# Pooled attention and a tanh-shrink layer: softmax with the row maximum, tokens on partitions, in place of keys on partitions

## The chip, the core and the metric

The kernel runs on one core of a Trainium2 chip. The metric is the device time of one execution in microseconds (us). The core has five engines with queues of their own: TensorE (PE) multiplies matrices, with the weight loads (PEld) beside it, VectorE (DVE) and ScalarE (ACT) work on rows, GpSimd (POOL) does the same more slowly, and SyncE (SP) issues most transfers. Sixteen DMA engines carry the transfers of all queues. PSUM, where matmuls write, has eight banks of 128 partitions by 512 fp32 columns.

## The reference

Inputs are q, k and v of shape (8 batches, 8 heads, 576 tokens, 64) and two weight matrices, 512 x 2048 and 2048 x 512, all fp32. What is computed, cut to its core:

```
k_p = k.reshape(B, H, 72, 8, D).mean(axis=3)        # 576 keys pooled to 72
v_p = v.reshape(B, H, 72, 8, D).mean(axis=3)
scores = q @ k_p.T / sqrt(D)
scores = scores - max(scores, axis=-1)
attn = exp(scores);  attn = attn / (sum(attn, axis=-1) + 1e-9)
x = (attn @ v_p)  ->  (B * S, H * D) = (4608, 512)
h = x @ w_in;  g = h - tanh(h);  out = g @ w_out
```

## The kernel before, in words

All matmuls take bf16 and add in fp32. The two large layers work in nine groups of 512 consecutive tokens (`TG`, `NG`). A group's **first layer** (`mlp_h_mms`, L448) makes 16 hidden blocks of 128: four matmuls of 512 columns each into one of three banks, w_in as weights and the transposed activations `xT` as moving operand. ACT takes tanh into `t_sb` (L464), and DVE subtracts it from the PSUM copy and writes `gT` (L466). The **second layer** (`mlp_o`, L475) takes four blocks of 128 tokens in turn, each 16 matmuls in four units of four; ACT copies the finished bank (L490) and SP stores it.

`xT` holds all 4608 tokens. A batch has 576, so groups and batches do not coincide: group g reads tokens of one or two batches, and the attention of batch g + 1 is worked out during group g.

Attention of one batch. The eight raw rows of each key are added in pairs, three adds (`pool_k`, L215; `pool_v`, L237), on POOL but for the first batches. 576 (head, key) rows lie in five tiles, and `KB` holds them so that one matmul serves two heads. **Scores have keys on partitions** (`score_mms`, L316): KB is the weight operand, the transposed queries `qT` move. ACT takes exp straight from PSUM into `E` (L340, L351), with the scale and without a maximum. `E` is then the weight operand of the matmuls with V (`av_mms`, L361), six of 130 columns for a block of 128 tokens. V has an extra column, so that the sum of weights comes out beside each head; DVE takes its reciprocal (L385) and multiplies (L386). The block `x_sb` is turned into `xT` by a DMA transpose (L403), or by TensorE (L409) in the first two batches.

The order is written out by hand: the schedule is manual, each engine runs its instructions in the order in which the program names them. During group g the program puts, between the second layer's units u = 0 to 15, the scores after u = 1 to 5, the blocks of x after u = 7, 8, 9, 10 and 12, and the cast and the five DMA transposes of the following batch's q after u = 12 (L809 to L823). Loads of the batch after next and the transpose of k come in the first layer (L796 to L808). SP's queue carries all these loads, transposes and stores in the same order.

Before group 0 comes an opening (L562 to L743). k, q and v of batch 0 arrive in pieces, POOL starts the loads of w_in and w_out that cast to bf16 (L526, L533), DVE pools k, TensorE turns k and q against `ident` (L282, L194) and runs matmuls on zeros (`warm_pe`, L548) in between. Scores and exp go tile by tile as k arrives. V of batch 0 is pooled by TensorE (L642). Then x of batch 0 is made in pairs of blocks (`av_pair`, L686; L692), turned by TensorE and copied to xT by ACT (`x0_turn`, L699; L712), and the first matmuls of the first layer (`h_open`, L717) take only half of the contraction, for which x is ready first. In group 0's second layer batch 1's k, q and x are turned by TensorE too (L768 to L786).

Of the kernel before, what the change touches and what calls it, by code (L numbers as in the profile page):

```python
# [11 lines left out]
ALU = mybir.AluOpType  # L12
PSUM = bass.MemoryType.PSUM

B, H, S, D = 8, 8, 576, 64
POOL = 8
# [6 lines left out]
T = B * S  # L23
# [3 lines left out]
NG = T // TG  # L27
NT = 5
D1 = D + 1
PR = 2 * G  # L30
LO = PR - 128
KP = 160
NM = 4
# [4 lines left out]
def kernel(  # L38
# [14 lines left out]
    raw = ctx.enter_context(tc.tile_pool(name="raw", bufs=2))  # L53
    work = ctx.enter_context(tc.tile_pool(name="work", bufs=2))
    gpool = ctx.enter_context(tc.tile_pool(name="gpool", bufs=1))
# [3 lines left out]
    PS = psum.tile([128, 8, 512], FP32, name="PS")  # L59

    def bank(i, shape):
        n = 1
        for d in shape[1:]:
            n *= d
        v = PS[:, i, 0:n]
        if len(shape) == 3:
            return v.rearrange("p (a b) -> p a b", a=shape[1])
        if len(shape) == 4:
            return v.rearrange("p (a b c) -> p a b c", a=shape[1], b=shape[2])
        return v  # L70

    class Banks:
        def __init__(self, *ids):
            self.ids, self.n = ids, 0

        def tile(self, shape, dtype=None, name=None, tag=None):
            self.n += 1
            return bank(self.ids[(self.n - 1) % len(self.ids)], shape)

    ps_h = Banks(0, 1, 2)  # L80
    ps_o = Banks(3, 4)
    ps_a = Banks(5, 6, 7)

    ctx.enter_context(tc.manual_schedule())
# [5 lines left out]
    k_pairs = k_rows.rearrange("b (t r) n -> b r t n", r=PR)  # L90
    v_pairs = v_rows.rearrange("b (t r) n -> b r t n", r=PR)

    w1b = const.tile([128, NFB, DFF], BF16, name="w1b")
    w2b = const.tile([128, NHID, DM], BF16, name="w2b")
    xT = const.tile([128, NFB, T], BF16, name="xT")
    ident = const.tile([128, 128], BF16, name="ident")
    spread = const.tile([128, 128], BF16, name="spread")
    mask = const.tile([128, 3 * NM, 1], FP32, name="mask")
    k_raw = [const.tile([128, NT, POOL * D], FP32, name=f"k_raw{i}") for i in range(2)]
    v_raw = [const.tile([128, NT, POOL * D], FP32, name=f"v_raw{i}") for i in range(2)]  # L100
    KB = [const.tile([128, NM * KP], BF16, name=f"KB{i}") for i in range(2)]
    q_bf = const.tile([128, R + 1, H, D], BF16, name="q_bf")
    warm = const.tile([128, 1], FP32, name="warm")
    x0 = const.tile([128, 4, 2, 4, D], BF16, name="x0")
    VB = [const.tile([128, 3 * NM, D1], BF16, name=f"VB{i}") for i in range(2)]

    q_raws = {}
    rot = [0]

    def ps_any(shape, dtype, name):  # L110
        pool, tag = [(ps_a, "ps_a"), (ps_h, "hT_ps")][rot[0] % 2]
        rot[0] += 1
        return pool.tile(shape, dtype, name=name, tag=tag)

    evac_n = [0]

    def evac(out, in_, eng=None):
        if (evac_n[0] % 2) if eng is None else eng == "act":
            nc.scalar.copy(out=out, in_=in_)
        else:  # L120
            nc.vector.tensor_copy(out=out, in_=in_)
        evac_n[0] += 1

    def load_main(src, dst, b, t0, t1):
        return nc.sync.dma_start(out=dst[:, t0:t1, :], in_=src[b, 0:128, t0:t1, :])

    def load_left(src, dst, b, eng=nc.sync):
        return [
            eng.dma_start(out=dst[32 * t : 32 * t + LO, NM, :], in_=src[b, 128:PR, t, :])
            for t in range(NM)  # L130
        ]

    def load_dense(src, dst, b, eng=nc.sync):
        return eng.dma_start(
            out=dst[0 : NM * LO, NM, :], in_=src[b, 128:PR, :, :]
        )

    def load_k(b):
        return [
            load_main(k_pairs, k_raw[b % 2], b, 0, NM),  # L140
            load_dense(k_pairs, k_raw[b % 2], b),
        ]

    def load_v(b):
        return [load_main(v_pairs, v_raw[b % 2], b, 0, NM)] + load_left(
            v_pairs, v_raw[b % 2], b
        )

    def load_q_tail(b, t, eng):
        eng.dma_start(  # L150
            out=t[:QT, :, R, :], in_=q[b, :, QA:S, :].rearrange("h p d -> p h d")
        )

    def load_q(b, tail=True):
        if b not in q_raws:
            q_raws[b] = raw.tile([128, H, R + 1, D], FP32, name="q_raw", tag="q_raw")
        t = q_raws[b]
        nc.sync.dma_start(
            out=t[:, :, 0:R, :], in_=q[b, :, 0:QA, :].rearrange("h (p j) d -> p h j d", j=R)
        )  # L160
        if tail:
            load_q_tail(b, t, nc.sync)

    qTs = {}
    kdups = {}

    def q_cast(b, eng=nc.gpsimd.tensor_copy, parts=1):
        t = q_raws.pop(b)
        n = H // parts
        for h in range(0, H, n):  # L170
            eng(  # L171
                out=q_bf[:, 0:R, h : h + n, :].rearrange("p j h d -> p h j d"),
                in_=t[:, h : h + n, 0:R, :],
            )
        eng(out=q_bf[:QT, R, :, :], in_=t[:QT, :, R, :])

    def q_dma_transpose(b):
        qT = work.tile([128, NHP, S], BF16, name="qT", tag="qT")
        for j in range(R + 1):
            rows = 128 if j < R else QT  # L180
            nc.sync.dma_start_transpose(
                out=qT[:, :, j * 128 : j * 128 + rows],
                in_=q_bf[:rows, j, :, :].rearrange("p h d -> p (h d)"),
            )
        qTs[b] = qT

    def q_pe_transpose(b, hps, eng=None):
        if b not in qTs:
            qTs[b] = work.tile([128, NHP, S], BF16, name="qT", tag="qT")
        qT = qTs[b]  # L190
        for hp in hps:
            ps = ps_any([128, QA], FP32, "qT_ps")
            for j in range(R):
                nc.tensor.matmul(  # L194
                    ps[:, j * 128 : (j + 1) * 128],
                    lhsT=q_bf[:, j, 2 * hp : 2 * hp + 2, :].rearrange("p h d -> p (h d)"),
                    rhs=ident[:, :],
                    start=True,
                    stop=True,
                )  # L200
            evac(qT[:, hp, 0:QA], ps[:, :], eng)

    def q_pe_tail(b):
        ps = ps_any([128, NHP, QT], FP32, "qt_ps")
        for hp in range(NHP):
            nc.tensor.matmul(
                ps[:, hp, :],
                lhsT=q_bf[:, R, 2 * hp : 2 * hp + 2, :].rearrange("p h d -> p (h d)"),
                rhs=ident[:, 0:QT],
                start=True,  # L210
                stop=True,
            )
        evac(qTs[b][:, :, QA:S], ps[:, :, :])

    def pool_k(b, eng, t0=0, t1=NT, mid=()):  # L215
        r = k_raw[b % 2].rearrange("p t (j d) -> p t j d", d=D)[:, t0:t1, :, :]
        if b not in kdups:
            kdups[b] = work.tile([128, NT, 2, D], BF16, name="kd", tag="kd")
        kd = kdups[b][:, t0:t1, :, :]
        n = t1 - t0  # L220
        first = eng.tensor_tensor(  # L221
            out=r[:, :, 0:4, :], in0=r[:, :, 0:4, :], in1=r[:, :, 4:8, :], op=ALU.add
        )
        for c in mid:
# [629 lines left out]
```

## Time and profile before

| what | value |
|---|---|
| time, three runs | 301.23 us median (300.78 to 301.84) |
| span of the profiled execution, first to last instruction | 299.0 us |
| time of that execution around its span | not given apart |
| PE busy | 291.5 us (97%), 1672 matmuls |
| PEld / DVE / ACT / POOL busy | 142.8 / 158.4 / 148.8 / 115.7 us |
| granted TensorE clock | 1.000 |
| mean DMA rate | 167 GB/s; 49.79 MB moved |
| DMA queue of SP and ACT's hardware (q1) | 55.5% of 16 engines' span |
| first matmul of the first layer | 18.35 us |
| first matmul of group 1's first layer | 54.87 us |
| last matmul of the second layer's last 128 tokens | about 295 us |

Busy time counts an instruction from its start to its end; matmuls overlap, so their mean duration (379 ns for 512 columns) is longer than the step from one to the next. "Idle before" in a group's line is the engine's idle time just ahead of such instructions, and what ended most of it. The chain is followed back from the last instruction to whatever released each step. SPq is SyncE's queue, with the time that an issue takes.

### The profile page before, as it was taken

To read this page: it belongs to the slowest core of one execution; us is meant where nothing else is said; L and a number is where in the kernel's file an instruction comes from. 1 tells how busy PE (TensorE), PEld (TensorE's weight loads), DVE (VectorE), ACT (ScalarE), POOL (GpSimd) and SP (SyncE) were. 2 spreads that over 40 slices of the span, in tenths; PEclk is the share of its full clock that TensorE was granted. 3 is DMA by queue.
4 is the path that set the end of the run, shared out by engine and by line. 5 is a ranking of instruction groups with operands and counts; after the bars stand their busy time and mean duration, and the time that the engine had idled before them with its cause. 6 is when DMAs were issued, how large, how long until landed. Compare 5 with 4: busy or idle time off the path is not lost.

```text
span 299.0 us, 4704 instructions
## 1 busy us (share of the span) xinstructions
PE 291.5 (97%) x1672; PEld 142.8 (48%) x1672; DVE 158.4 (53%) x336; ACT 148.8 (50%) x279; POOL 115.7 (39%) x110
## 2 busy tenths in 40 slices
PE   7999999999999999999999999999999999999994
PEld 3454355544544454445544554455445544444443
DVE  5658665673547444753476247715680758008600
ACT  4647583666146623664266416651666066126511
POOL 8600906770396109913971099208930000000000
PEclk9999999999999999999999999999999999999999
DMA  7999999749955995699648974895431630111033
GB/s 259 221 211 280 310 235 328 233 89 331 233 109 109 290 283 129 109 297 250 105 89 236 313 166 88 265 294 137 89 66 35 90 96 0 37 70 36 2 70 70
DMA packets 66183, 49.79 MB, mean 167 GB/s; under 512 B 39920, under 2 KB 52976, under 8 KB 66160
## 3 DMA queue, kind: packets, MB, share of 16 engines
q1 hardware_dynamic: 58832, 42.94, 55.5%
q0 software_dynamic: 4752, 4.72, 9.5%
q10 hardware_dynamic: 2576, 1.84, 2.2%
q8 instruction: 13, 0.21, 0.3%
q14 instruction: 10, 0.08, 0.1%
HBM read 36.70 MB, written 9.44 MB: 154 GB/s over the span
## 4 chain that ended last, share of the span: by engine, by line
PE 85%; DMA 9%; POOL 4%; issue 0%; SPq 0%; ACT 0%; DVE 0%; POOLq 0%; DVEq 0%
PE PS L481 40%; PE PS L453 37%; DMA w1b<-in_moe_w_in_dram 4%; PE PS L368 4%; DMA k_raw<-in_k_dram 4%; PE PS L321 3%; POOL k_raw L221 1%; DMA out_dram<-o_sb 1%; POOL k_raw L226 1%; POOL kd L229 1%; POOL w2b L535 0%; PE PS L416 0%; POOL v_raw L599 0%; PE PS L194 0%; POOL w1b L528 0%
## 5 line engine op out<-in xcount | busy, mean ns | idle before, releaser
L481 PE MATMUL PS<-w2b,gT 128*128 128x512 bf16 x560 | 134.3, 379 | 0.0
L466 DVE TENSOR_TENSOR gT<-PS,t_sb 128x512 bf16<-128x512 f32 x144 | 98.9, 691 | 56.9 <-ACT t_sb L464 56.7
L453 PE MATMUL PS<-xT,w1b 128*128 128x512 bf16 x576 | 126.8, 379 | 0.6 <-ACT xT L712 0.6
L464 ACT ACTIVATE t_sb<-PS 128x512 f32<-128x512 f32 x144 | 85.6, 597 | 38.5 <-PE PS L453 37.7
L453 PEld LDWEIGHTS <-w1b 128*128 128x128 bf16 x576 | 55.9, 98 | 67.3 <-issue 0.8
L481 PEld LDWEIGHTS <-gT 128*128 128x128 bf16 x560 | 52.5, 98 | 52.0 <-issue 1.4
L490 ACT COPY o_sb<-PS 128x512 f32<-128x512 f32 x33 | 19.3, 586 | 75.2 <-PE PS L481 75.2
L385 DVE RECIPROCAL rden<-PS 128x4 f32<-128x4 f32 x72 | 12.8, 177 | 52.6 <-PE PS L368 52.3
L171 POOL CAST q_bf<-q_raw 128x2048 bf16<-128x2048 f32 x6 | 11.3, 1890 | 60.2 <-issue 34.2
L386 DVE TENSOR_TENSOR x_sb<-PS,rden 128x256 bf16<-128x256 f32 x72 | 30.6, 424 | 2.9 <-DMA xT<-x_sb 0.4
L221 POOL TENSOR_TENSOR k_raw<-k_raw 128x1280 f32<-128x1280 f32 x7 | 20.2, 2887 | 26.5 <-DMA k_raw<-in_k_dram 26.5
L340 ACT ACTIVATE E<-PS 128x288 bf16<-128x288 f32 x60 | 21.4, 409 | 13.2 <-PE PS L321 13.0
L368 PEld LDWEIGHTS <-E 128*128 128x128 bf16 x240 | 16.8, 98 | 8.3 <-issue 0.4
L368 PE MATMUL PS<-VB,E 128*128 128x130 bf16 x240 | 20.2, 220 | 0.1
L239 POOL TENSOR_TENSOR v_raw<-v_raw 128x1280 f32<-128x1280 f32 x6 | 17.4, 2900 | 0.0
L321 PE MATMUL PS<-qT,KB 128*128 128x288 bf16 (+5 forms) x128 | 17.0, 289 | 0.2
L321 PEld LDWEIGHTS <-KB 128*128 128x128 bf16 (+1 forms) x128 | 7.0, 96 | 10.2 <-issue 3.5
L550 PE MATMUL PS<-xT 128*128 128x512 bf16 x30 | 10.4, 463 | 1.3 <-DVE xT L562 1.3
L229 POOL TENSOR_TENSOR kd<-k_raw 128x640 bf16<-128x640 f32 x7 | 10.8, 1539 | 0.5
L226 POOL TENSOR_TENSOR k_raw<-k_raw 128x640 f32<-128x640 f32 x7 | 10.8, 1542 | 0.5
L242 POOL TENSOR_TENSOR v_raw<-v_raw 128x640 f32<-128x640 f32 x6 | 9.2, 1538 | 0.5
L272 POOL COPY KB<-kT 64x288 bf16<-64x288 bf16 x6 | 2.5, 418 | 13.8 <-DMA kT<-kd 13.8
(78 smaller groups left out, 107.1 us busy)
## 6 DMA issues: line engine op xcount, KB each, us to landing
k_raw<-in_k_dram SPq DMA_DIRECT2D x7, 1024.0 KB, 5.9
q_raw<-in_q_dram SPq DMA_DIRECT2D x7, 1024.0 KB, 10.2
v_raw<-in_v_dram SPq DMA_DIRECT2D x7, 1024.0 KB, 9.2
out_dram<-o_sb SPq DMA_DIRECT2D x38, 128.0 KB, 2.4
out_dram<-o_sb SPq DMA_DIRECT2D x16, 256.0 KB, 2.8
w1b<-in_moe_w_in_dram POOLq DMA_DIRECT2D x4, 512.0 KB, 13.7
w2b<-in_moe_w_out_dram POOLq DMA_DIRECT2D x4, 512.0 KB, 16.8
k_raw<-in_k_dram SPq DMA_DIRECT2D x7, 128.0 KB, 5.9
```

The source lines that it names most:

```text
L221: first = eng.tensor_tensor(out=r[:, :, 0:4, :], in0=r[:, :, 0:4, :], in1=r[:, :, 4:8, :], op=ALU.add)
L226: eng.tensor_tensor(out=r[:, :, 0:2, :], in0=r[:, :, 0:2, :], in1=r[:, :, 2:4, :], op=ALU.add)
L239: eng.tensor_tensor(out=r[:, :, 0:4, :], in0=r[:, :, 0:4, :], in1=r[:, :, 4:8, :], op=ALU.add)
L321: nc.tensor.matmul(dst[p : p + w], lhsT=KB[b % 2][:, o : o + w], rhs=qTs[b][:, m, c0:c1], start=True, stop=True,)
L340: nc.scalar.activation(out=E[:, t, half * hs : (half + 1) * hs], in_=ps[:, :], func=ACT.Exp, scale=SCALE)
L368: nc.tensor.matmul(ps[:, 2 * n : 2 * n + 2, :].rearrange("p h d -> p (h d)") if n < 2 else ps.rearrange("p (a s) d -> p a s d", s=2)[:, :, ...
L386: nc.vector.tensor_tensor(out=x_sb[:, half, :, :], in0=ps[:, :, 0:D], in1=rden[:, :, :].to_broadcast([128, 4, D]), op=ALU.mult,)
L453: nc.tensor.matmul(h_tiles[i][:, :], lhsT=w1b[:, fb, i * 128 : (i + 1) * 128], rhs=xT[:, fb, tok0 : tok0 + TG], start=(fb == 0), stop=(fb ...
L464: nc.scalar.activation(out=t_sb[:, :], in_=h_ps[:, :], func=ACT.Tanh)
L466: nc.vector.tensor_sub(out=gT[:, :], in0=h_ps[:, :], in1=t_sb[:, :])
L481: nc.tensor.matmul(o_ps[:, :], lhsT=gts[i][:, tb * 128 : (tb + 1) * 128], rhs=w2b[:, i, :], start=(i == 0), stop=(i == NHID - 1),)
L490: (nc.vector.tensor_copy if g == 0 and tb % 2 else nc.scalar.copy)(out=o_sb[:, :], in_=o_ps[:, :])
```

## The change

Most of the kernel is written anew; inputs, outputs, types, the pooling, the two layers' matmuls and the last 128 tokens' split store stay.

- **Groups.** Groups 0 to 7 are the first 512 tokens of one batch each; group 8 is the last 64 tokens of all eight batches. `xT` of all tokens becomes two buffers of 512 tokens in turn, and `xTt` for group 8. Tails of q are loaded, cast, turned and worked on for two batches together (`s_tail`, `av_tail`), in the group before an odd batch.
- **Scores** have tokens on partitions: `qT` is the weight operand, `KB` (144 columns for two heads) moves; four matmuls for 128 tokens, into two banks.
- **Row maximum.** DVE takes the maximum over 72 keys (L249) and subtracts it, from PSUM into an fp32 tile in SBUF (L252); ACT takes exp of that tile (L260).
- **Weights turned.** The matmul with V needs the weights with keys on partitions: a DMA transpose of 128 x 640 on SP's queue turns them (L273), in batch 0 TensorE and an ACT copy (L276).
- **V** matmuls are of 130, 195 and 65 columns (table `AV`); one reciprocal and one multiplication serve a whole block of 128 tokens, two banks at once.
- **Casts and turns.** The cast of q goes from POOL to ACT, in two pieces; one DMA transpose turns the 512 tokens of q, where there were five. Batch 1's q, k and first three x blocks are turned by DMA and not by TensorE.
- **Banks and order.** The first layer cycles through six banks (three before). The second layer's units are reordered, so that the last gT tiles are read later. Scores start in the first layer of the group, and the last block of x comes after unit 10, the tail after unit 13.
- **Opening.** The first layer of group 0 goes in halves of 256 tokens, two hidden blocks to a bank, and starts when two blocks of x are there. All of k is placed before the first scores. 28 matmuls on zeros stand in the opening (`fill`), 30 before.

```diff
+    def s_mms(unit, banks):
+        for ps, qT, kb in unit:
+            for m in range(NHP):
+                nc.tensor.matmul(PS[ps, banks[m // 2], KP * (m % 2) : KP * (m % 2) + KP],
+                    lhsT=qT[:, m, :], rhs=KB[kb][:, m, :], start=True, stop=True)
+    def s_shift(banks):
...
+        nc.vector.reduce_max(out=mx.rearrange("p k h o -> p k (h o)"), in_=sc, axis=AX.X)
+        nc.vector.tensor_tensor(out=sh[:, :, :, :], in0=sc,
+            in1=mx.to_broadcast([128, 2, 4, G]), op=ALU.subtract)
+    def s_exp(sh):
...
+        nc.scalar.activation(out=E[...], in_=sh[...], func=ACT.Exp, scale=SCALE)
+    def e_turn_dma(E):
...
+        nc.sync.dma_start_transpose(out=ET[:, :, :], in_=E.rearrange("p t c -> p (t c)"))
+    AV = ((0, 0, 1, 3), (0, 1, 0, 3), (0, 2, 0, 1), (1, 2, 1, 3), (1, 3, 0, 3), (1, 4, 0, 1))
+    def h_mm_pair(n, half, bank):   # group 0: 256 tokens, two hidden blocks
+        for s in range(2):
+            for fb in range(NFB):
+                nc.tensor.matmul(PS[:, bank, 256 * s : 256 * s + 256],
+                    lhsT=w1b[:, fb, (2 * n + s) * 128 : (2 * n + s + 1) * 128],
+                    rhs=xT_of(0)[:, fb, c0 : c0 + 256], ...)
 # opening
+    k_turn_pe(0, 4, NT, kps)
+    fill(10, 7)
+    k_turn_pe(0, 2, 4, kps)
+    k_place(0, kps[:, 0:NK], (ve, se))
+    q_turn_pe(0, 0, 6, se)
+    q_turn_pe(0, 1, 7, se)
...
+    for m, (n, half) in enumerate(seq):
+        h_mm_pair(n, half, bk)
+        h_act_pair(n, half, bk)
+        if 4 <= m < 8:
+            q_cast(1, se, m - 4, m - 3)
+        if m == 7:
+            q_turn_dma(1)
 # groups 1 to 8: s = scores and shift, e = exp and turn, a = matmul with V, normalise, turn of x
+    UNITS = [(0, 0), (0, 1), (0, 2), (1, 0), (1, 1), (0, 3), (1, 2), (1, 3)]
+    UNITS += [(tb, qd) for tb in (2, 3) for qd in range(4)]
+            plan = {-10: [("s", 0)], -7: [("e", 0)], -5: [("s", 1)], 0: [("e", 1)],
+                1: [("s", 2)], 2: [("s", 3)], 3: [("e", 2)], 5: [("a", 0), ("e", 3)],
+                6: [("a", 1)], 8: [("a", 2)], 10: [("a", 3)]}
+            if tail:
+                plan[4] = [("s", 4)]
+                plan[6].append(("e", 4))
+                plan[8], plan[9] = [], [("a", 2)]
+                plan[13] = [("a", 4)]
```

A plan's key is the unit of the second layer after which the step stands; negative keys count hidden blocks of the first layer before its end (-10 is the seventh block). Group 1 has a later plan (`s` from -2 on). Loads of the batch after next are issued after hidden blocks 0 to 5, k, q and the tails are turned after unit 12, and pooling k begins after unit 0.

## The prediction

> **What bounds the kernel now.** I read first the chain of work that ended last, then TensorE's own waits, then the chain in order of time, then the timeline of the opening.
>
> ```profile
> PE 85%; DMA 9%; POOL 4%; issue 0%; SPq 0%; ACT 0%; DVE 0%; POOLq 0%; DVEq 0%
> ```
> ```profile
> PE PS L550 <- DVE xT L562: 1.3, 1, 1.3
> PE PS L282 <- POOL kd L229: 0.7, 1, 0.7
> PE PS L453 <- ACT xT L712: 0.6, 1, 0.6
> ```
> TensorE (PE) carries the chain; the second fence is its waits (total, times, longest), and after the opening there are none. The chain in time shows the beat:
>
> ```profile
> 116.64 13.81 PE PS L453 x64
> 130.45 1.73 PE PS L481 x8
> ...
> 147.45 13.81 PE PS L453 x64
> ```
> From one first-layer block (64 matmuls of 512 columns in 13.81 us, 0.2158 each) to the next are 30.81 us: 13.81 for the first layer, 13.81 for the second, so 3.19 for one batch's scores and weights times V. Groups 1 to 6 have this beat; groups 7 and 8 (from 239.87) are pure matmul. So a change can gain or lose only TensorE work, the opening, or waits that it brings back into the beat. The opening:
>
> ```profile
> 14.60 1.20 PE L368 MATMUL PS<-VB,E 128*128 128x130 bf16 x18
> 15.38 0.69 DVE L692 TENSOR_TENSOR x<-PS,rden 128x512 bf16<-128x512 f32 x1
> 17.23 1.07 ACT L712 CAST xT<-PS 128x512 bf16<-128x512 f32 x2 [3.48 <-PE PS L368]
> 18.35 0.59 PE L453 MATMUL PS<-xT,w1b 128*128 128x512 bf16 x2 [0.55 <-ACT xT L712]
> ```
> The first layer opens at 18.35 us; from there TensorE never rests. Group 0 ends at 54.87 (group 1's first L453): 36.5 us.
>
> **Prices.** From the groups of instructions:
>
> ```profile
> L466 DVE TENSOR_TENSOR gT<-PS,t_sb 128x512 bf16<-128x512 f32 x144 | 98.9, 691 | 56.9 <-ACT t_sb L464 56.7
> L386 DVE TENSOR_TENSOR x_sb<-PS,rden 128x256 bf16<-128x256 f32 x72 | 30.6, 424 | 2.9 <-DMA xT<-x_sb 0.4
> L340 ACT ACTIVATE E<-PS 128x288 bf16<-128x288 f32 x60 | 21.4, 409 | 13.2 <-PE PS L321 13.0
> ```
> DVE: 424 ns at 256 elements and 691 at 512, so 1.04 ns an element: a 576-element subtraction is 0.76 us, a 960-element one 1.16. ACT: 409 at 288 and 597 at 512: a 576-element exp is 0.65, a 640-element copy 0.70. The row maximum is in no row: 0.76 as the subtraction (same input), as little as half of that if a reduction streams faster, up to 1.5 if it streams at half speed. I take 0.76, the nearest row.
>
> ```profile
> 25.70 0.28 PE L206 MATMUL PS<-ident,q_bf 128*128 128x64 bf16 x4
> 25.95 0.38 PE L453 MATMUL PS<-xT,w1b 128*128 128x512 bf16 x1
> ```
> Four 64-column matmuls with new weights take 0.25 us, 62 ns each, though their columns alone are 27. Six of 130 columns (29.77 to 30.11) take 57 each. Small matmuls have a floor near 60 ns.
>
> **The change, part by part.**
>
> Scores and V, groups 1 to 6. Scores: per 128 tokens 4 matmuls of 144 columns, 0.25. V: 6 of 130, 195 or 65 columns: 57, 85 and 62 ns, twice: 0.40. Four blocks are 2.6. In batches 3, 5 and 7 a tail of two batches adds 8 score and 12 V matmuls, 1.3. Six batches: 6 x 2.6 + 3 x 1.3 = 19.5, against 6 x 3.19 = 19.1: +0.4 (-0.7 if the 65-column ones cost only their columns and halves of the array overlap, +1.5 if each costs 70 ns).
>
> DVE in those groups. Two score units fall in the first layer: 16 x 0.691 + 4 x 0.76 = 14.1 us, beside 13.81 + 0.5 of TensorE. That just fits; six banks (three before) and the order of the second layer, which needs the last four gT tiles only five units (4.3 us) in, cover the lag. In the second layer DVE has some 8 us of work. ACT takes exp, stores and the cast of q (1.04 each, twice) from POOL: under 0.5 of its time. Cost 0 while that cover holds.
>
> DMA and SyncE's queue. Four to five turns of weights (160 KB) per batch are new; turns of x (4 or 5 of 128 KB), one of k, and one 512 KB turn of q stand for the old 11.
>
> ```profile
> 87.30 6.44 SPq L181 DMA_TRANSPOSE qT<-q_bf  x5
> ...
> 95.55 1.20 SPq L304 DMA_TRANSPOSE kT<-kd  x1
> ```
> A turn holds SyncE's queue for 1.2 us whether it is 128x512 or 128x640, and lands 2.5 us after its issue. SP per batch: about 11 x 1.2 + 7 loads and 4 stores x 0.6 = 20 of 30.8 us. DMA share of the beat, by stretches, is 0.77; q's turns (576 KB in 58 to 64 us at 0.45) give 0.6 us of all engines per 128 KB, so weights add 4.5 x 0.75 = 3.4 us: 0.88. What is behind what: after the unit that ends the first store (call that 0) SP issues in order the store, x block 0 (waits for its DVE normalise, 1.55), weights 3 (2.75), x 1 (3.95), in odd batches the tail's weights, the second store, x 2, x 3. Weights 3 land near 5.2; TensorE reaches the matmuls that read them at 5.5. x 3 lands at 9.5 (10.6 in odd batches); the next group's first layer, which now needs all four blocks at once, starts at 10.2 (11.0). Slack 0.3 to 0.7 us, where the old kernel worked up to a batch ahead. I charge 0.1 us a group, 0.6 in all; bounds 0 and 1 us a group (6).
>
> The opening, the largest term. Times are from the old landings: k's first half by 5.3, the rest by 8.0. DVE pools 0:2 (1.54), tile 4 (1.0), 2:4 (1.54) until 9.6. Ahead of the last turn of k stand 10 filling matmuls, from 8.05: 10 x 0.2158, so it starts at 10.25. KB is placed by DVE (0.45) and then ACT (0.42), in turn: 11.55. ACT copies q 0 (12.15) and q 1 (12.75). Scores 12.2 to 12.65; maximum and subtraction to 14.25; exp to 14.95; PE turn and ACT copy of the weights to 16.2. Then ACT is the chain: exp 1, q 2, weights 1, q 3 to 18.75, because scores of block 2 need the bank that q 3 leaves. x of blocks 0 and 1 is in xT at 21.65: the half-width first layer opens at 21.7, not 18.35. It does 5 of 16 half-steps (0.87 each) while blocks 2 and 3 go through the same hops (maximum until 23.6, exp 24.65, weights 25.95, normalise 28.5, copy 29.6); from 29.65 the other 11 run on: 39.15. In 21.7 to 29.65 TensorE works 6.2 us and idles 1.75. Second layer of group 0: 13.81 + scores and tail 1.5 + V 1.6 + V pooled by TensorE 8 x 0.136 + x turn 0.2 = 18.25: 57.4, against 54.87: **+2.5**. All steps are sequential by rows; each engine hand-over counts 0.05, so the error is +-2.
>
> Turn of q in group 0: cast by ACT until 38.2, one 128x2048 turn. Issue 1.2 and little more by the two rows above, and 512 KB at 2.4 us of all engines: lands about 42.4, needed at 39.15 + 4 x 0.863 = 42.6. If it were four 128x512 turns one after the other, 4 x 1.29 + 1.3, it lands at 44.7: 2.1 late. I take +0.5. k of batch 1 is loaded after the second piece of w1, at about 16 instead of 18.45, so its pool on POOL is done some 5 us before it is wanted: 0.
>
> [...]
>
> The end (last 128 tokens split 384 and 128, two stores each) is the same in both: 0.
>
> **Sum.** 2.5 + 0.5 + 0.4 + 0.6 = +4.0 on the span of 299.0: 303.0. The profiled execution's own time is not given apart; the runs shown are 300.78 to 301.84, so 1.8 to 2.8 us lie around the span, 2.2 at the median. Forecast: **305.2 us**.
>
> **Rivals.**
> 1. Faster. From the first layer's opening to the end of group 0 the changed kernel has less for TensorE: 14.0 + 13.8 + 1.8 (rest of batch 0) + 4.4 = 34.0 us against 36.5, since q, k and three x blocks of batch 1 are turned by DMA. So the opening wins from the point where opening plus idle is under 20.9 us, 20.5 with the +0.4 above. If hops overlap (the maximum at half price, KB placed at once, no filling ahead of k) and it opens at 19.0 without holes, group 0 ends at 53.0: -1.9 + 0.4: 299.7 us. Against: 14 dependent hops on three engines, of which the old opening had 9.
> 2. A wait in every group: x block 3 or weights 3 land late, because the turns queue behind one another on SP and beside stores. 1 us a group: +5.4 more, 310.6. For: slack of 0.3 to 0.7; one old x turn took 4.6 to land. Against: the median is 2.5.
> 3. DVE becomes the bound: with the maximum at 1.5 us a unit, DVE has 15.6 us in a 14.3 us first layer, and weights come later by 0.75 a unit: about 1 us a group and 1.5 in the opening: 312.
> 4. The opening without holes, no late turn: group 0 ends at 55.7: +0.8 + 0.4: 302.4.
>
> TensorE's clock in the opening: matmuls before 5.3 us take 0.43 each, later 0.2158. [...]
>
> **How the numbers follow.** Forecast (303 to 308) 0.53; rival 2 0.18; rival 3 0.07; rival 4 0.10; rival 1 0.12. About 0.3% (0.9 us) can be told from no change here. Rival 4 lies half within it, and a sliver of the forecast: same 0.09. Faster 0.13, slower 0.78. The range leaves out most of rival 1 and the far end of 2 and 3: 300.3 to 312.
>
> **What would show it.** First half-width L363 matmul near 21.7, last near 39; group 1's first layer near 58; then a beat of 30.3 and 31.6 us in turn (27.62 + 2.6 or 3.9, and 0.1), with nothing but DMA or DVE as releaser if longer. Row maximum 0.76. PE L363 waiting on ACT or DVE for about 2 us in sum. I am wrong if the first layer opens before 20, if the beat holds waits of over 0.5 us, or if small matmuls run under 55 ns.

## The result, and the profile after

The changed kernel takes 331.0 us (median of four runs, 327.94 to 331.87), the one before 301.1 beside it: a ratio of 1.097 (95% interval 1.092 to 1.102). The forecast was 305.2 with a range of 300.3 to 312. The direction held; the loss of 30 us is seven times the forecast's 4. The profiled execution took 331.36 us with a span of 329.6, so 1.8 us lie around the span.

The page's chain of work that ended last, shares by engine:

```profile
PE 55%; DMA 36%; ACT 2%; SPq 2%; issue 1%; DVE 1%; POOL 0%; ACTq 0%
```
TensorE carried 85% of it before and carries 55% now; transfers went from 9% to 36%. TensorE's own waits name them (total us, times, longest):

```profile
PE PS L299 <- DMA ET<-E: 9.5, 6, 4.8
PE PS L344 <- DMA xT<-x_sb: 4.7, 5, 2.1
PE PS L235 <- DMA qT<-q_bf: 4.0, 3, 3.5
PE PS L220 <- DVE kd L163: 3.4, 3, 1.7
```
The first three are turns by DMA: of weights, x and q. After the opening the old kernel had no such line. Where the time is lost is read from the start of each group's first layer in TensorE's timeline:

| stretch | before, us | after, us | difference |
|---|---|---|---|
| start to group 0's first layer | 18.35 | 24.57 | +6.2 |
| group 0 (to group 1's first layer) | 36.5 | 44.4 | +7.9 |
| group 1 | 30.8 | 41.0 | +10.2 |
| groups 2 to 6 | 154.0 | 160.7 | +6.6 |
| groups 7, 8 and the end | 59.3 | 59.0 | -0.3 |

**Group 0.** The chain in order of time (start, duration, what), between 20 and 62 us:

```profile
20.96 18.88 DMA q_raw<-in_q_dram
...
43.52 6.56 DMA qT<-q_bf
...
52.88 8.77 DMA ET<-E
```
The load of batch 1's q takes 18.9 us beside the loads of the MLP's weights and v; its casts end at 43.5; its turn takes 6.56 us, and the first turn of weights 8.77. (In the old kernel the same load took 16.3 us and landed at 36.3.) TensorE's timeline shows what follows:

```profile
50.13 0.72 PE L235 MATMUL PS<-KB,qT 128*128 128x144 bf16 x8 [3.47 <-DMA qT<-q_bf]
50.64 3.57 PE L384 MATMUL PS<-w2b,gT 128*128 128x512 bf16 x8
```
After 3.47 us of waiting, eight matmuls of 512 columns take 3.57 us, where eight elsewhere take 1.89: half speed, and a granted clock of 0.51 from 50.6 to 54.1. A wait of 1.58 for weights follows, until 61.70.

**Group 1.** SyncE's queue (start, duration of the issue):

```profile
75.03 6.12 SPq L214 DMA_TRANSPOSE qT<-q_bf  x1
81.19 0.59 SPq L112 DMA_DIRECT2D k_raw<-in_k_dram  x1
...
87.73 5.08 SPq L273 DMA_TRANSPOSE ET<-E  x2
```
The turn of batch 2's q holds the queue for 6.12 us (median of all seven 1.84). The loads of batch 3 queue up behind it and go out together from 81.2 to 87.6, just ahead of the first turn of weights, which then needs 9.20 us. TensorE waits 4.82 us for it, until 96.98, and again runs eight matmuls in 3.60. A wait of 2.12 for x closes the group. The turn in the chain, and TensorE's wait:

```profile
87.73 9.20 DMA ET<-E
```
```profile
96.98 0.84 PE L299 MATMUL PS<-VB,ET 128*128 128x130 bf16 x6 [4.82 <-DMA ET<-E]
```
The windows of the trace give the load on the engines. A line has the window, its length, the busy time of PE, PEld, DVE, ACT and POOL, then granted clock, DMA share and GB/s. The share is the time of all packets over that of 16 engines, so it can pass 1. The changed kernel:

```profile
20.00:40.00 20.00, 17.96 (x182) 14.75 (x183) 12.26 (x21) 11.63 (x21) 7.24 (x5) 1.00 1.17 248
43.50:50.10 6.60, 3.16 (x14) 1.07 (x12) 2.70 (x5) 1.96 (x4) 2.06 (x5) 1.00 1.02 159
52.80:61.70 8.90, 7.32 (x41) 3.58 (x39) 4.95 (x7) 2.10 (x4) 3.79 (x2) 0.93 1.10 271
72.00:97.00 25.00, 19.80 (x112) 9.33 (x111) 16.50 (x25) 13.80 (x24) 13.55 (x8) 0.96 1.10 261
120.00:131.00 11.00, 11.00 (x72) 5.53 (x70) 10.09 (x16) 5.30 (x10) 5.98 (x3) 1.00 1.07 261
110.00:270.00 160.00, 155.32 (x900) 75.80 (x899) 105.75 (x172) 80.22 (x131) 64.77 (x44) 1.00 0.80 187
```
The kernel before:

```profile
20.00:40.00 20.00, 18.99 (x118) 9.17 (x116) 13.09 (x25) 14.02 (x25) 7.48 (x5) 1.00 1.15 276
72.00:97.00 25.00, 25.00 (x147) 12.31 (x146) 13.30 (x32) 12.10 (x24) 15.26 (x10) 1.00 0.72 167
```
Where the late turns land, the DMA share is 1.0 to 1.2 (1.24 from 38.1 to 47.8, where k's turn stands). The old kernel's stretch from 20 to 40 us was as full (1.15), but there it had no turn by DMA at all: its first is at 57.7 us, and TensorE did those of batch 1. From 110 us on the changed kernel has 0.80 on average, but the average hides the loads of each group: from 120 to 131 it is 1.07, and the first turn of weights of groups 2 to 5 takes 7.9, 9.5, 9.3 and 9.7 us. TensorE waits for only one of these four, 0.41 us, since they are issued in the first layer, well before it reads them; in group 1 the plan issues the turn later. So a late landing costs only what goes beyond the distance to its reader.

**Groups 2 to 6.** Visible waits sum to 5.3 of the 6.6 us: 1.19, 0.30, 0.50, 0.41, 0.19, 0.17, 1.01 and 1.48, all on turns. Groups with a tail (2, 4 and 6) have beats of 33.1, 32.2 and 33.0, the others 30.7 and 31.7.

**Opening.** DVE's timeline, then POOL's:

```profile
11.11 0.42 DVE L160 TENSOR_TENSOR k_raw<-k_raw 128x256 f32<-128x256 f32 x1
11.57 1.95 DVE L163 TENSOR_TENSOR kd<-k_raw 128x256 bf16<-128x256 f32 x1
```
```profile
10.64 1.53 POOL L135 DMA_DIRECT2D w1b<-in_moe_w_in_dram  x2 [1.26 <-DMA k_raw<-in_k_dram]
12.15 1.07 POOL L208 CAST q_bf<-q_raw 128x1024 bf16<-128x1024 f32 x1
```
DVE waits for the last piece of k until 10.38, 2.4 us later than I reckoned. The last add of k then takes 1.95 us and not the 0.42 of an add of that size; it ends 0.3 us after POOL's cast of q. So k's last turn starts at 13.57, not 10.25. The ten fills ahead of it would have held it nearly as long: they take 0.43 us each, twice the price that I gave them, and end at about 13.2.

The DVE prices, from the page's groups, are as forecast:

```profile
L249 DVE TENSOR_REDUCE mx<-PS 128x8 f32<-128x576 f32 x36 | 27.1, 752 | 10.6 <-PE PS L235 10.5
L252 DVE TENSOR_TENSOR sh<-PS,mx 128x576 f32<-128x576 f32 x36 | 27.3, 758 | 1.3
```

### The profile page after: what moved, and what is told of

It is laid out like the page before. It is cut to its first block, busy times and chain, and to the rows that moved or that the text cites. A ratio compares the mean times of both kernels' runs of the same rounds, so it can differ in the third digit from the quotient of the medians.

```text
span 329.6 us, 4754 instructions
## 1 busy us (share of the span) xinstructions
PE 298.8 (91%) x1737; PEld 149.9 (45%) x1737; DVE 191.6 (58%) x315; ACT 149.8 (45%) x249; POOL 108.2 (33%) x94
## 3 DMA queue, kind: packets, MB, share of 16 engines
q10 hardware_dynamic: 2240, 1.18, 1.4%
## 4 chain that ended last, share of the span: by engine, by line
PE 55%; DMA 36%; ACT 2%; SPq 2%; issue 1%; DVE 1%; POOL 0%; ACTq 0%
PE PS L344 26%; PE PS L384 24%; DMA ET<-E 12%; DMA q_raw<-in_q_dram 8%; DMA qT<-q_bf 6%; DMA xT<-x_sb 4%; PE PS L299 3%; DMA w1b<-in_moe_w_in_dram 3%; DMA k_raw<-in_k_dram 3%; PE PS L235 2%; ACT q_bf L208 1%; DMA out_dram<-o_sb 1%; SPq L118 1%; DVE mx L249 0%; SPq L405 0%
## 5 line engine op out<-in xcount | busy, mean ns | idle before, releaser
L384 PE MATMUL PS<-w2b,gT 128*128 128x512 bf16 (+2 forms) x592 | 138.1, 381 | 0.0
L344 PE MATMUL PS<-xT,w1b 128*128 128x512 bf16 x448 | 99.8, 380 | 4.7 <-DMA xT<-x_sb 4.7
L260 ACT ACTIVATE E<-sh 128x576 bf16<-128x576 f32 x36 | 24.2, 681 | 27.2 <-DVE sh L252 27.2
L249 DVE TENSOR_REDUCE mx<-PS 128x8 f32<-128x576 f32 x36 | 27.1, 752 | 10.6 <-PE PS L235 10.5
L299 PE MATMUL PS<-VB,ET 128*128 128x130 bf16 (+4 forms) x240 | 20.3, 227 | 9.5 <-DMA ET<-E 9.5
L252 DVE TENSOR_TENSOR sh<-PS,mx 128x576 f32<-128x576 f32 x36 | 27.3, 758 | 1.3
L318 DVE TENSOR_TENSOR x_sb<-PS,rden 128x512 bf16<-128x512 f32 x36 | 24.9, 692 | 1.4 <-DVE rden L317 0.2
L299 PEld LDWEIGHTS <-ET 128*128 128x128 bf16 (+1 forms) x240 | 15.7, 103 | 20.3 <-DMA ET<-E 14.4
L208 ACT CAST q_bf<-q_raw 128x1024 bf16<-128x1024 f32 (+1 forms) x19 | 16.5, 866 | 6.9 <-DMA q_raw<-in_q_dram 6.9
L363 PE MATMUL PS<-xT,w1b 128*128 128x256 bf16 x128 | 14.9, 273 | 1.5 <-DVE gT L376 0.8
```

The lines of the kernel that those rows point to most:

```text
L208: eng(out=q_bf[b % 2][:, j0:j1, :, :].rearrange("p j h d -> p h j d"), in_=q_raw[b % 2][:, :, j0:j1, :],)
L249: nc.vector.reduce_max(out=mx.rearrange("p k h o -> p k (h o)"), in_=sc, axis=AX.X)
L252: nc.vector.tensor_tensor(out=sh[:, :, :, :], in0=sc, in1=mx.to_broadcast([128, 2, 4, G]), op=ALU.subtract)
L260: nc.scalar.activation(out=E.rearrange("p t c -> p (t c)")[:, 0:NK], in_=sh.rearrange("p k h c -> p (k h c)"), func=ACT.Exp, scale=SCALE,)
L299: nc.tensor.matmul(PS[ps, banks[half], D1 * h : D1 * (h + s1 - s0)], lhsT=ET[:, t, c0 : c0 + (ps.stop - ps.start)], rhs=VB[kb][:, t, s0:s1 ...
L318: nc.vector.tensor_tensor(out=x_sb[:, :, :, :], in0=ps[:, :, :, 0:D], in1=rden.to_broadcast([128, 2, 4, D]), op=ALU.mult,)
```

## The experiments

**Theory:** turns by DMA are cheap only while the sixteen engines have room. In groups 0 and 1 they run beside loads, many land in 6 to 9.6 us, and TensorE waits. **Rivals:** (A) the longer chain over DVE (maximum, subtraction) makes the weights late; (B) what is queued ahead of a turn on SyncE's queue does it, so another queue for the loads or stores cures it; (C) the hand-over is too tight in any case, loads or not. Ratios are to the kernel before, with 95% intervals; medians are of four runs.

### One part alone, in the old kernel

The old kernel, with k and q of batch 1 turned by DMA instead of TensorE, and the loads of batch 2 behind those turns:

```diff
+    k_dma_transpose(1)          # after pool_k(1)
+    k_place(1, nc.gpsimd.tensor_copy)
...
+            q_dma_transpose(1)  # second layer of group 0, after u == 0
+            after(load_k(2), w2_dmas[2])
+            load_v(2)
+            load_q(2)
-        if u == 2:
-            k_transpose(1, ps_any, (nc.vector.tensor_copy, nc.vector.tensor_copy))
-        if u == 3:
-            q_pe_transpose(1, (0, 1), "act")
```


> The kernel before, with one part of the change alone: k and q of batch 1 turned by DMA (k placed by POOL), the loads of batch 2 issued behind the turn of q. Theory A: turns land after 5 to 9 us instead of 2.5 while w_out is loading; TensorE waits at the first scores of batch 1 for 3 to 8 us: 304 to 309. Theory B (DMA turns are hidden): 300 to 302, since TensorE loses 2 us of turns.

Measured: 309.71 us, 1.027 (1.022 to 1.032): 8.9 us lost. TensorE's timeline and SyncE's queue:

```profile
47.84 0.58 PE L321 MATMUL PS<-qT,KB 128*128 128x512 bf16 x1 [9.04 <-DMA qT<-q_bf]
```
```profile
37.82 1.31 SPq L304 DMA_TRANSPOSE kT<-kd  x1
39.23 7.82 SPq L181 DMA_TRANSPOSE qT<-q_bf  x5
```
One wait of 9.04 us, with half speed until about 50.5 (three matmuls of 512 columns in 1.48 us from 48.65), makes the loss: group 0 ends at 63.29, not 54.87, and every later group takes what it took before. No row maximum, no turned weights and no new opening is needed for it. It shows that turning q and k by DMA at this place costs 8.9 us, where I had put 0.5. It does not show that slow landings are the larger part: the casts of q end at 39.2, TensorE comes for q at 38.8, and at the prediction's own price (4 x 1.29 + 1.3) the four turns that it waits for would land at 45.7. They land at 47.7. By this estimate 2 of the 9 us are slow landings, and 7 are that the turns begin only when TensorE is already there.

### Undone in the changed kernel: k and q of batch 1 by TensorE

```diff
-    k_turn_dma(1)
...
-            q_turn_dma(1)
+        if u == 0:
+            k_turn_pe(1, 0, NT, kp1)
+            k_place(1, kp1[:, 0:NK], (ve, ve))
+        if u == 1:
+            q_turn_pe(1, 0, 2, se)
+            q_turn_pe(1, 1, 3, se)
+        if u == 2:
+            q_turn_pe(1, 2, 0, se)
+            q_turn_pe(1, 3, 1, se)
```


> k and q of batch 1 are turned by TensorE in group 0's second layer (k after unit 0, q after units 1 and 2, ACT and DVE copies), as the kernel before did, in place of two DMA turns. Theory A (turns in the time when w_out, k, q and v are still loading are late): TensorE's wait of 3.5 us at 46.7 to 50.1 and the half-speed matmuls behind it go, against 1.2 us of turns: 3 to 5 us faster, 327. Theory B: the casts of q, which wait for the landing at 39.8, hold TensorE instead: no gain, 331.

Measured: 327.78, 1.085 (1.079 to 1.092). The wait for q is gone, but the next turn takes its place:

```profile
62.05 0.84 PE L299 MATMUL PS<-VB,ET 128*128 128x130 bf16 x6 [4.84 <-DMA ET<-E]
62.70 1.90 PE L384 MATMUL PS<-w2b,gT 128*128 128x512 bf16 x4
```
The weights of batch 1 now arrive 4.84 us late, and four matmuls take as long as eight should. Only 3 us are won, and not where I expected them: in the profiled execution (330.25, the slowest of four) group 0 takes 46.4 us, 2 more than in the changed kernel, and group 1, which the edit leaves alone, 37.6 for 41.0. That the total is near the 327 expected is luck.

Carried on (weights of batches 1 and 2 by TensorE too; group 1's part is shown, in group 0 the units are moved likewise and V of batch 1 is placed earlier):

```diff
-                ets[n] = e_turn_dma(s_exp(shs[n]))
+                if g == 1:
+                    pend.append((n, s_exp(shs[n]), (2, 6, 0, 2)[n]))   # e_turn_pe two units later
...
+                else:
+                    ets[n] = e_turn_dma(s_exp(shs[n]))
```


> In groups 0 and 1 no turn that TensorE needs soon goes by DMA: k, q and the weights of batch 1 and the weights of batch 2 are turned by TensorE, each at least one unit behind its exp (x, batch 2's q and k still by DMA; groups 2 to 6 as in the changed kernel). Theory A (the 31 us are mostly turns that share the DMA engines with the first loads): group 0 ends near 62 instead of 69, group 1 takes 33 to 34 us instead of 41, the rest stays: 315 to 318 us. Theory B (the order of the units is what costs): over 325.

Measured: 325.49, 1.082 (1.080 to 1.085). Group 0 takes 41.8 us and group 1 35.4 (44.4 and 41.0 in the changed kernel). The expected 315 to 318 us did not come. With no turn by DMA that TensorE needs soon, group 0 is still 5.2 us longer than before and group 1 4.6; so taking them out wins 2.7 of the 7.9 us of group 0 and 5.6 of the 10.2 of group 1, at this order of units. What is left in group 0 is the late load of q, its casts, and waits of 2.63 us on DVE and 0.73 on the load of v. Groups 2 to 6, which the edit leaves alone, take 162.9 us, 2.2 more; why is not known.

### Taking the loads away

The loads of batches 3 to 7 left out, so that old data are used again (V of batch 1 is cleared whole in their place):

```diff
-        todo = load_list(nb + 1, nc.sync) if more else []
+        todo = []
```


> The loads of batches 3 to 7 are left out (old data are pooled, turned and used again); turns, stores and all engine work stay; V of batch 1 is cleared whole in between. Theory A (turns by DMA are late because loads occupy the same 16 engines): weights' turns land after 2.5 to 3 us at the median, group 1 falls from 41.0 to 33 us or less, groups 2 to 6 to 30.1 (even) and 31.1 (odd) each: 315 us. Theory B (turns and SyncE's issues are slow by themselves): waits stay, 328 or more.

Measured: 321.96, 1.067 (1.062 to 1.072). The landing of the four turns of weights of group 1, in the changed kernel and then here:

```profile
DMA to landing us min/median/max: 2.4/6.0/9.2
```
```profile
DMA to landing us min/median/max: 2.4/2.4/2.4
```
Group 1 takes 33.1 us, 7.9 less; groups 2 to 6 take 158.9, only 1.8 less. So loads make most of the loss of group 1. Rival C is right in groups 2 to 6: without loads waits stay there (1.17, 0.87, 1.26 us on turns), and so the total lies between the 315 and the 328 us that the two theories gave.

The loads of k and q of batch 2 left out, which POOL issues beside the weights' turns of group 0:

```diff
-    for ld in load_list(2, nc.gpsimd)[:3]:
-        ld()
```


> The loads of k and q of batch 2, which POOL issues at 50 to 52 us, are left out (batch 0's are used again); nothing else changes. Theory A: the four turns of batch 1's weights then land after 2.5 to 4 us instead of up to 8.8, TensorE's wait of 1.6 us at 60 and its half-speed steps go: 2 to 4 us faster, 328. Theory B (turns slow by themselves): 331.

Batch 0's k and q are used again. Measured: 329.0, 1.095 (1.092 to 1.098). The four turns of weights in group 0, in the changed kernel and then here:

```profile
DMA to landing us min/median/max: 3.7/6.9/8.8
```
```profile
DMA to landing us min/median/max: 2.4/2.4/4.4
```
From 48 to 56 us, where these loads are issued, the DMA share falls from 0.68 to 0.37, and the wait of 1.58 for weights is gone:

```profile
60.84 0.34 PE L299 MATMUL PS<-VB,ET 128*128 128x130 bf16 x3
```
This is the clearest sight of the cause: the same turns, at the same place, land in 2.4 us when those loads are away. The total shows little of it. The median is 2 us lower, within the two intervals. In the profiled execution (326.63, the fastest of four) group 0 takes 40.6 us (44.4), but q's wait was 2.59 us there and no half speed followed it, which the edit does not explain; group 1 keeps 39.9.

### Moving the loads

The last three quarters of w_out and v of batch 1 later, so that q of batch 1 comes sooner:

```diff
     load_w2(0)
-    load_w2(1)
-    load_rows(v_rows, v_bf[1], 1, eng=nc.gpsimd)
-    load_w2(2)
-    load_w2(3)
...
+        if mid:
+            mid()      # the same four, after the first add of pool_k(1)
```


> The second to fourth piece of w_out and v of batch 1 are issued by POOL after the first add of pooling k of batch 1, not in the opening. Theory (transfers): in the opening q of batch 1 was issued at 21.0 us and landed at 39.8 because w_out and v shared the 16 engines; it should now land by 34, its turn should be ready before 43, the wait of 3.5 us of TensorE at 46.7 to 50.1 and the half-speed matmuls behind it (1.8 us) go: about 6 us faster than the changed kernel, 325. Rival (the row maximum on DVE makes the chains long): no change, 331. [...]

Measured: 334.45, 1.111 (1.109 to 1.113). q lands in 13.7 us instead of 18.9, but the postponed loads then meet the turns: k's takes 9.1 and q's 9.3 us, and TensorE waits 7.15 until 52.68. (The profile puts this wait down to POOL, but q's turn is what lands at 52.6.) The gain I expected did not come: q's load lands 4 us sooner, but its turn starts at 43.36 as before, behind k's, which is issued at 41.86 and not at 38.10, and it takes 2.7 us more.

Loads of the later batches on ACT's queue (q10 in the trace of the changed kernel, where its 1.18 MB are what ACT issues; q1 is SyncE's alone), so that no turn stands behind a load (rival B):

```diff
-    for ld in load_list(2, nc.sync)[3:]:
+    for ld in load_list(2, nc.scalar)[3:]:
...
-        todo = load_list(nb + 1, nc.sync) if more else []
+        todo = load_list(nb + 1, nc.scalar) if more else []
```


> The loads of later batches (k, q, v, tails, from batch 2's v on) are issued by ACT, so on its own DMA queue; SP keeps turns and stores. Theory (a turn waits for everything ahead of it on SP's DMA queue): the weights' turns land after 2.5 us at the median, not 3.7, and none after 9; the waits of 4.8 us in group 1 and about 1 us in each of groups 2 to 6 go: 10 us faster, 321. Rival (the 16 engines are simply full while loads run): turns still land after 5 to 9 us in those stretches, 0 to 3 us faster. Rival (row maximum): no change.

Measured: 365.52, 1.203 (1.192 to 1.214). Its profiled execution was the slowest of its four (370.84), so its places are read here and not its total. q's turns (least, median, greatest time to landing), in this kernel and then in the changed one:

```profile
DMA to landing us min/median/max: 4.3/9.0/16.7
```
```profile
DMA to landing us min/median/max: 4.3/4.4/8.1
```
The turns of weights, likewise:

```profile
DMA to landing us min/median/max: 2.4/2.4/8.3
```
```profile
DMA to landing us min/median/max: 2.4/3.7/9.7
```
With loads on a queue of their own, the turns of weights land sooner (2.4 us at the median for 3.7, as expected), but those of q take twice as long (9.0 for 4.4), and TensorE waits 12.5, 9.6, 4.5 and 3.4 us for them: the loads now start right behind the issue of q's turn, at 118.8 us for a turn issued at 117.67. So a place of its own in a queue moves the collision and does not remove it. ACT pays too: it spends up to 4.16 us on the issue of two loads between its own instructions. Rival B fell as a cure in this form; that the order on the queue matters, it shows.

Stores of groups 1 to 6 on ACT's queue:

```diff
-            nc.sync.dma_start(out=dst, in_=o_sb[r0:r1, :])
+            (nc.scalar if 0 < g < 7 else nc.sync).dma_start(out=dst, in_=o_sb[r0:r1, :])
```


> In groups 1 to 6 the stores of the output are issued by ACT, on its own DMA queue; SP keeps turns and loads. Open: groups 2 to 6 take 160.7 us in the changed kernel, 153.4 by their matmuls' steps; without the loads they took 158.9. Theory C (SP's queue, in order and 1.2 us a turn, hands the last weights and the last x on too late): four issues of 0.5 us and their waits leave it, the tail's weights and x block 3 land about 1 us earlier: groups 2 to 6 fall by 3 to 5 us, 327. Rival D (the turns themselves are slowed by the stores on the shared engines): no change, 331.

Measured: 335.45, 1.114 (1.110 to 1.117). TensorE waits 13.5 us for weights (9.5 in the changed kernel), and groups 2 to 6 take 164.7 us, 4 more. The turns of q land in 6.0 us at the median, not 4.4. Both expectations (327 and 331) failed; as a cure rival B fell here too.

### No row maximum

exp straight from PSUM, neither maximum nor subtraction:

```diff
-        nc.vector.reduce_max(...)
-        nc.vector.tensor_tensor(out=sh[...], in0=sc, in1=mx..., op=ALU.subtract)
-        return sh
+        return sc
```


> Without row maximum and subtraction: exp reads PSUM directly. DVE loses 54 us of work. Rival (the row maximum is what costs): 15 us faster or more, near 315. Theory (transfers): only the dependent hops shorten: 1.5 to 3 us at the opening, up to 1.5 in group 0; waits for late turns stay: 3 to 4 us faster, 327.

Measured: 331.87, 1.102 (1.098 to 1.106), the same as with it. 1.5 us less per unit and 54 us less of DVE buy nothing, not even the 3 to 4 us that I expected, so rival A fell.

### No turns of weights by DMA

Weights turned by TensorE and an ACT copy in every batch, one unit after the exp was issued (in groups 2 to 6 the second scores stand one hidden block later):

```diff
-                ets[n] = e_turn_dma(s_exp(shs[n]))
+                pend.append((n, s_exp(shs[n]), t_banks[n]))
...
+            n, E, b0 = pend.pop(0)
+            ets[n] = e_turn_pe(E, b0, se)
```


> From batch 1 on the weights are turned by TensorE (five 128-column matmuls, then an ACT copy of 640 columns), one unit after the exp, not by DMA; the second scores of groups 2 to 6 stand one hidden block later. TensorE gets 32 x 5 x 57 ns = 9 us more, ACT 22 us. Theory (turns land late behind loads): waits for weights (9.5 us and half-speed matmuls after them) and part of the x waits go, so the sum is 0 to 4 us faster than the changed kernel, 327 to 331, with groups 2 to 6 at 33 us each. Rival (the turns are not late, the chain on DVE and ACT is): 9 us slower, 340.

Measured: 335.46, 1.114 (1.111 to 1.116). Waits on ET are gone, but TensorE now waits for ACT's exp (8.9 us in 13 waits), and groups 2 to 6 take 167.0, 6.3 more. By an estimate from the expectation's price (5 x 57 ns a turn, 23 turns in these groups) 6.6 us of that are the turns' own matmuls, so the waits were exchanged and not removed. At this distance it is no cure; a longer distance was tried only in groups 0 and 1 (above).

### The opening

Cast of q's second half by ACT, V loaded after all of k, and 4 fills for 10:

```diff
-    q_cast(0, ge, 2, 4)
+    q_cast(0, se, 2, 4)
...
-eng=nc.gpsimd), k0[0])
+eng=nc.gpsimd), k0[1])
-    fill(10, 7)
+    fill(4, 7)
```


> Opening only: the second half of q of batch 0 is cast by ACT and not by POOL, the load of V waits for all of k, and 4 filling matmuls stand ahead of the last turn of k, not 10. Theory A (in group 0 the transfers set the end): the first layer opens 1.5 to 2 us earlier than 24.57, since the add of k that took 1.95 us beside POOL's cast takes 0.42, but the turn of q of batch 1 still lands at 50: total 330 to 331, unchanged. Theory B (the opening adds to the end directly): 329.

Measured: 334.72, 1.112 (1.105 to 1.118). k's turn starts at 11.93, 1.6 sooner, but TensorE waits 1.87 us for V, until 16.93, and the first layer opens at 26.70, later than in the changed kernel.

The same without moving V:

> Opening only, with V's load where the changed kernel has it: the second half of q of batch 0 cast by ACT, 4 filling matmuls ahead of the last turn of k. The last add of k takes 0.42 and not 1.95 us, the first layer opens near 23, 1.4 us earlier. Theory A: q of batch 1 still lands at 39 to 40, so at most a third of that reaches the end: 330 to 331. Theory B (the opening adds directly): 329.5.

Measured: 332.24, 1.105 (1.100 to 1.109). The last add is back at its price:

```profile
11.62 0.43 DVE L163 TENSOR_TENSOR kd<-k_raw 128x256 bf16<-128x256 f32 x1
```
POOL issues its loads beside it here too (3.01 us from 10.69), so it was the cast, not the issue, that drew it out. The first layer opens at 23.86, 0.7 sooner, and the end does not move: TensorE meets batch 1's q at about 50 all the same. What is won is spent waiting: ACT stands 5.56 us before the cast of q, its tanh behind it, and TensorE waits 2.84 us at 43.12 for gT (0.78 in the changed kernel).

Then q's second half loaded behind k instead of beside it:

```diff
-    load_q(0, q_raw[0], 2, 4, nc.scalar)
+    load_q(0, q_raw[0], 2, 4, nc.sync)
```


> e11 (cast of q's second half by ACT, 4 filling matmuls), and q's second half is loaded behind all of k on SP's queue, not beside it on ACT's. Open: why the first layer opens 6.2 us later than in the kernel before. Theory E (scores with tokens on partitions need every key, so they wait for k's last piece at 10.4): k's last piece lands near 8.8, the first scores come 1.5 us earlier than in e11 and the first layer opens near 22.5; the total stays at 330 to 332, since q of batch 1 still lands near 40 and its cast holds ACT. Rival: the hops behind the scores set the opening, 23.9 as in e11.

Measured: 330.23, 1.095 (1.091 to 1.099). The last add now starts at 9.91, 1.7 sooner, so q beside it made 1.7 of the 2.4 us by which k was late. The first layer opens at 22.75, 1.8 sooner than in the changed kernel. The total is the same within the runs: the wait for q's turn at 50.4 stays.

### Mends together

TensorE's turns in groups 0 and 1, the opening of two experiments before, and v and tails of batch 2 loaded behind the turn of its q:

```diff
             if g == 1 and i == 3:
                 q_turn_dma(2)
+                for ld in load_list(2, nc.sync)[3:]:
+                    ld()
```


> e10 and e11 together, and batch 2's V and tail are loaded behind the turn of batch 2's q, not ahead of it. Theory A: e10's gain, 1.4 us of the opening and some of group 1's wait for q: 313 to 316 us, still above the kernel before, since the opening (about 5 us) and the waits of groups 2 to 6 (about 6) stay.

Measured: 321.41, 1.068 (1.066 to 1.069), the fastest version with the change, but not the 313 to 316 expected. Against the kernel before, its profiled execution loses 5.1 us in the opening, 6.4 in group 0, 3.3 in group 1 and 6.2 in groups 2 to 6. With stores on ACT's queue and q behind k as well:

> e13, e14 and e15 together. If the parts add up: 321.4 less 3 to 4 for the stores less 0.5 for the opening: 317 us, slower than the kernel before by 5%; more than 321 if the stores on ACT's queue hold up TensorE through ACT.

Measured: 323.53, 1.074 (1.071 to 1.077): no better, where 317 was expected. None of these beats the kernel before.

## Why the prediction was wrong

- **The step that failed** is the landing of turns in groups 0 and 1: "a turn lands 2.5 us after its issue", and for batch 1's q "lands about 42.4". I took the price from rows of the old kernel's beat, at a DMA share of 0.77, and used it where the share is 1.0 to 1.2. There, turns take 6.6 (q), 8.8 and 9.2 (weights) and 9.6 us (k, hidden behind q's). Without those loads the same turns of weights land in 2.4 at the median. The old kernel had no row for it, because TensorE did every turn before 57.7 us. I should have bounded this from above by q's load of batch 1 in the same stretch, not by a quiet row.
- **In the same step, q's cast:** I had it end at 38.2, from the old landing of q's load at 36.3; the load landed at 39.84 and the casts ended at 43.5. Of the 7.7 us by which q is late (50.08 against 42.4), this is 5.3 and the turn itself 2.4.
- **Missed term, group 0:** +7.9 against -0.3 (35.7 from the opening to the end, and 0.5 for q's turn, for the old 36.5). The waits of 3.47 and 1.58, the half-speed matmuls (1.7) and waits of 0.78 and 0.65 make 8.2. That loads make the weights late is shown by leaving the loads out. That turns by DMA cost the whole of it is not shown: with those of k, q and the weights on TensorE 5.2 us stay.
- **Missed term, group 1:** +10.2 against about 0.2. Waits of 4.82, 2.12 and 0.38 and half-speed matmuls of 1.7 make 9.0. Without loads 7.9 of it vanish, and the turns of weights land in 2.4 us.
- **Hand-over, mis-sized:** 0.1 us a group forecast; groups 2 to 6 show 5.3 us of waits and take 6.6 more than before. Rival 2 had the place and nearly the price (1 us a group); its mechanism, turns queueing beside stores, is not shown. Loads explain 1.8 of it. The rest stays open: neither stores on another queue nor, at one unit's distance, TensorE's turns removed it.
- **Opening, mis-sized:** 24.57 against 21.7. k landed 2.4 late, 1.7 of it since q's second half came beside it, and the last add cost 1.5 more beside POOL's cast. Both are shown by undoing them, with 4 fills for 10 in the same runs. Undone, 22.75 is left, within my +-2. "10 x 0.2158" for the fills was wrong as well, hidden behind the late k: they take 0.43 each.
- **Right:** maximum 0.75 us (0.76 forecast), subtraction 0.76, exp 0.68 (0.65), DVE no bound, the end about 0 (-0.3 with groups 7 and 8). The attention's matmuls were +0.4 in the sum; groups 2 to 6 without TensorE's waits take 155.4 us against 154.0, an upper bound of +1.4 for them, since holes too short to be listed are still in it.
- **The price of q's turn.** I reckoned "issue 1.2 and little more". A turn of 128x2048 holds SyncE's queue for 1.84 us at the median of seven and lands in 4.4; those of x, 128x512, hold it for 1.22 and land in 2.4 at the median of 27. So the queue's time did grow with size here, but by 1.5 for four times the size, not fourfold.
- **The clock.** I reckoned with 1.75 us of idling in the opening, and my sum has no price for half speed. Three later holes were longer than 2 us. After the two longest (3.47 and 4.82) eight matmuls took 3.57 and 3.60 us, where eight elsewhere take 1.89, at a granted clock of 0.51 and 0.50. After the third (2.12, until 109.93) the clock was 1.00. What failed was my reckoning of the holes.

## What to carry to other kernels

A DMA transpose had no single price here: the same 128x640 turn landed in 2.4 us or in 9.2, by what was loaded beside it. So read the DMA share by stretches at the places where new ones will stand, doubt every landing time taken from a quieter one, and then ask how long before its reader the turn is issued. If an old kernel spends TensorE time on something that a DMA could do, look at what fills the DMA engines just there. Where one late hand-over is mended and the next one takes its place, as here from q to weights, only the sum over the chain counts.

## What else the runs showed of the hardware

- Half speed did not go by the length of a TensorE wait alone. Waits of 2.12 (changed kernel), 2.34 (q behind k), 2.59 (k and q of batch 2 left out), 2.63 and 2.65 (TensorE's turns in groups 0 and 1, and the first mends together) and 2.92 us (stores on ACT's queue) were followed by full speed; waits of 2.64 (stores on ACT's queue), 2.77 and 3.16 (no turns of weights by DMA), 3.32 (no loads) and 3.47 (changed kernel) by half speed, at once or within about a microsecond. With the stores on ACT's queue both are in one run: after 2.92 us the granted clock was 1.00 (50.2 to 54.0), after 2.64 it was 0.62 on average (61 to 65). What decides it, no run here shows.
- An addition on DVE with both inputs in SBUF took 1.95 us beside a cast on POOL, and 0.43 without the cast while POOL issued loads. The cast's own record is 1.07 us long.
- At the very start, and for the ten fills at 8.78, matmuls of 512 columns take 0.43 us each while the profile gives a granted clock of 1.00; at 50.6 and 97.6 the same pace comes with 0.51 and 0.50. So in the opening the pace is read from the matmuls.
